# One large store of zeros written as two large and fifteen small stores, ahead of the last group's dv store

## The chip, the cores and the metric

The kernel runs on one core of a Trainium2 chip. The metric is the device time of one execution in microseconds; the median of the runs is compared. The core has five engines that work side by side: TensorE (PE in the profile) for matrix products, VectorE (DVE), ScalarE (ACT), GpSimd (POOL) and SyncE (SP), which here only issues transfers. Transfers between the main memory (HBM) and the on-chip memory (SBUF) are DMAs; sixteen DMA engines of the core carry them out.

## The reference

A decode step of one token for four sequences: layer norm, then in parallel an attention over a window of a key/value cache and a gated feed-forward network, both added to the input. The kernel computes the output and the gradients of all inputs for a given gradient of the output.

```python
def ref(x, k_cache, v_cache, wq, wo, w_gate, w_up, w_down):   # x: (4, 1, 512)
    xn = layernorm(x)
    W = 1024                                   # of 4096 cached positions, the last ones
    q = heads(xn @ wq)                         # 32 query heads of 128, 8 key/value heads
    k, v = last(k_cache, W), last(v_cache, W)  # (4, 8, 1024, 128), each shared by 4 heads
    o = softmax(q @ k.T * 128**-0.5) @ v
    a = o @ wo
    b = (gelu(xn @ w_gate) * (xn @ w_up)) @ w_down
    return x + a + b
out, vjp = jax.vjp(ref, ...)
return (out, *vjp(grad_out))
```

The gradients of the caches, dk and dv, have the caches' full shape (4, 8, 4096, 128) in bf16, 33.6 MB each. Outside the window of the last 1,024 positions they are zero, so three quarters of each, 3,072 positions per sequence and head, are zeros that still have to be written: 50.3 MB of the 81.0 MB that the kernel writes.

## The kernel before

The feed-forward part comes first: its weights are loaded, transposed by TensorE, and its weight gradients computed and stored from tiles named osb_d and osb_g. Then the attention runs in a loop over four groups t of two key/value heads each (NT = 4, GP = 2). For a group, `kv_steps` transposes the keys (later the values) and forms the scores, `softmax` and `softmax_d` work out the softmax and its gradient in pieces, `odq` computes the outputs and the query gradients, and `fin` adds to the sums for the output and for dx. The key and value gradients of a group are made by `dvdk` (tiles stg_dv, stg_dk), those of the two attention weights by `dw` (tiles osb_o, osb_q). These last two are cut into pieces: a product, a copy out of PSUM (line 97 on ScalarE, line 98 on VectorE) and, with the last piece of a tile, a store. The pieces wait in a queue `bg`; `tick(n)`, called between the steps of the main path, runs n of them. What is left over after the last group is run by `tick(len(bg))`, line 754 before the change.

The order of the instructions on every engine is the order of the program text; nothing is moved by a scheduler. All large stores are issued by SyncE through `store` (lines 100 to 107). A store of dv or dk waits until its tile is filled, and while it waits, SyncE issues nothing that comes after it. The tile pool `stage` holds three stg tiles of 8 KB in each partition; each tile is 1 MB. A fourth tile takes the place of the first, and so its filling waits until the first one's store has landed. Per group four such tiles are made: two of dv, two of dk.

The zeros come from one SBUF tile, ztile, 128 partitions of 12 KB. `zero(n)` takes n entries off `zlist` and writes for each a region of one sequence and two heads: 128 rows of 12 KB, 1,536 KB. There are 32 such regions. They are spread over the program as filling for the DMA engines: three at the start, single ones after other stores (each dv and dk store is followed by one, line 490), four in a row in the last group (lines 733 and 734), and what remains at the end (line 755).

Semaphores are set by the framework. For hardware DMAs it uses eight completion counters in turn, for SyncE's and ScalarE's DMAs together in the order of the program. A DMA that takes a counter for the next time first waits until the DMA that had it before, the eighth before it, has landed. In the compiled program every store on SyncE from the ninth DMA on has such a wait. The two small results, out_b (line 769) and dx_b (line 787), are stored by ScalarE.

Around the change SyncE's order is: the two osb_q stores of group 2, the four zero stores, the first dv store of group 3, a zero store, the second dv store, a zero store, the first dk store, a zero store, osb_o, the second dk store, a zero store, osb_o, two osb_q, and two zero stores that end the program.

Of the kernel before, what the change touches and what calls it, by code (L numbers as in the profile page):

```python
# [14 lines left out]
P = 128  # L15
# [3 lines left out]
def kernel(  # L19
# [28 lines left out]
    nc = tc.nc  # L48

    B, Sq, D = A_x.shape  # L50
    _, G, Sk, Dh = A_k_cache.shape
# [4 lines left out]
    K0 = Sk - W  # L56
# [43 lines left out]
    def store(eng, out, in_, kind):  # L100

        eng.nop()
        d = eng.dma_start(out=out, in_=in_)
        for k in ("rest", "zeros") if kind == "rest" else ("rest",):
            tc.declare_no_dep(d.ins, group=k, reason="stores write disjoint parts of the outputs")
        tc.add_to_no_dep_group(kind, d.ins)
        return d
# [12 lines left out]
    def load_w(t, eng=nc.gpsimd):  # L120
        pool = w_pool[t % 2]
        wo_t[t] = pool.tile([P, HG, D], BF16, name="wo_sb", tag="wo")
        eng.dma_start(out=wo_t[t][:], in_=wo_v[t])
        wq_t[t] = pool.tile([P, ND, CW], BF16, name="wq_sb", tag="wq")
        eng.dma_start(out=wq_t[t][:], in_=wq_v[t])

    def load_kv(t, k):
        if t >= NT:
            return
        d_, src, nm = ((k_t, A_k_cache, "kb"), (v_t, A_v_cache, "vb"))[k]  # L130
        for g in range(GP):
            tl = kv_pool[t % 2].tile([P, JB, Dh], BF16, name=nm, tag=nm)
            nc.sync.dma_start(out=tl[:].rearrange("p j d -> p (j d)"),
                              in_=src[:, t * GP + g, K0:Sk, :].rearrange("b (m j) d -> m b (j d)", j=JB))
            d_[(t, g)] = tl
# [20 lines left out]
    ZR = 2  # L156
    ZW = K0 * Dh * ZR // P
    ztile = const.tile([P, ZW], BF16, name="ztile")
    zlist = deque((og, b, g) for b in range(B) for g in range(0, G, ZR) for og in (out_2, out_3))

    def zero(n=1):
        for _ in range(min(n, len(zlist))):
            og, b, g = zlist.popleft()
            store(nc.sync, og[b, g:g + ZR, 0:K0, :].rearrange("g (m j) d -> m g (j d)", m=P // ZR), ztile[:], "zeros")


    nc.gpsimd.memset(ztile[:], 0.0)
    zero(3)
    ident_f = const.tile([P, P], FP32, name="ident_f")
    nc.vector.tensor_copy(out=ident_f[:], in_=ident[:])  # L170
# [91 lines left out]
    def tick(n):  # L262
        for _ in range(min(n, len(bg))):
            bg.popleft()()
# [3 lines left out]
    def link(n=1):  # L268
        for _ in range(min(n, len(chain))):
            chain.popleft()()  # L270
# [64 lines left out]
    def kv_steps(t, k, links):  # L335

        zt = (qm_all, dom_all)[k][t % 2]
        blks = (k_t, v_t)[k]
        ps = ps_a.tile([P, WQ], FP32, name="S_ps", tag=("S", "dP")[k])
        st[t][("S", "dP")[k]] = ps[:]  # L340

        def mm(g, q, T_sb):
            c0 = SL - 1 - (g * NQ + q)
            for b in range(B):
                nc.tensor.matmul(ps[b * RB:(b + 1) * RB, :], lhsT=zt[:, b * GP + g, c0:c0 + RB],  # L345
                                 rhs=T_sb[:].rearrange("p (x b) -> p b x", b=B)[:, b, :], start=(g == 0 and q == 0),
                                 stop=(g == GP - 1 and q == NQ - 1), tile_position=(0, b * RB))

        last = None
        for g in range(GP):  # L350
            for q in range(NQ):
                T_ps = transposes([blks[(t, g)][:, q * JQ + j, :] for j in range(JQ)], "T")
                T_sb = tsb.tile([P, JQ * P], BF16, name="T_sb", tag="T")
                evac(T_sb[:], T_ps[:].rearrange("p j x -> p (j x)"), 1024, half=True)
                tick(1)
                link(links)
                if last:
                    mm(*last)
                last = (g, q, T_sb)
                tick(1)  # L360
                link(links)
        mm(*last)
# [104 lines left out]
    def odT(t, k):  # L467
        rows = st[t][("o", "dq")[k]]
        T_ps = transposes([rows[:, g, :] for g in range(GP)], "odT")
        rT = attw.tile([P, GP, B, rep], BF16, name="od_T", tag=f"od_T{k}")  # L470
        for g in range(GP):
            nc.vector.tensor_copy(out=rT[:, g].rearrange("p b r -> p (b r)"), in_=T_ps[:, g, g * 32:g * 32 + B * rep])
        st[t][("oT", "dqT")[k]] = rT
# [206 lines left out]
    for f4 in range(NF4):  # L680
        held = {}
        n = min(4, NF - 4 * f4)
# [34 lines left out]
    with tc.tile_pool(name="kv_b", bufs=GP, reuse_waits="tile") as kv_b, \  # L717
            tc.tile_pool(name="w_b", bufs=1, reuse_waits="tile") as w_b, \
            tc.tile_pool(name="stage", bufs=3, reuse_waits="tile") as stage:
        kv_pool[1], w_pool[1] = kv_b, w_b  # L720
        zero()
        pre(0)
        load_w(1)
        load_kv(1, 0)
        for t in range(NT):
            kv_steps(t, 0, 0)
            if t == 0:
                zero()
                load_kv(1, 1)
                zero()  # L730
            softmax(t)
            kv_steps(t, 1, 1)
            if t == NT - 1:
                zero(4)
            link(len(chain))
            softmax_d(t)
            link()
            odq(t, 0)
            load_kv(t + 2, 1)
            if t + 1 < NT:  # L740
                pre(t + 1)
            link(len(chain))
            odT(t, 0)
            odq(t, 1)
            load_kv(t + 2, 0)
            tick(2)
            odT(t, 1)
            fin(t)
            if t + 2 < NT:
                load_w(t + 2)  # L750
            (k0, k1), (o0, o1, q0, q1) = dvdk(t, 1), dw(t)
            for p in (k0, o0, k1, o1, q0, q1):
                bg.extend(p)
        tick(len(bg))
        zero(len(zlist))

        fin_ps = []
        for o in range(2):
            f_ps = ps_w.tile([B, ND, P], FP32, name="f_ps", tag="w")
            for c in range(ND):  # L760
                nc.tensor.transpose(f_ps[:, c, :], acc[:, o, c, :], ident_f[:])
            fin_ps.append(f_ps)
        acc_o = fin_ps[0][:].rearrange("b c p -> b (c p)")
        acc_d = attw.tile([B, P, ND], FP32, name="acc_d", tag="P_s")
        nc.vector.tensor_copy(out=acc_d[:].rearrange("b p c -> b c p"), in_=fin_ps[1][:])
        acc_d = acc_d[:].rearrange("b p c -> b (p c)")
        out_b = attw.tile([B, D], BF16, name="out_b", tag="pT")
        nc.vector.tensor_tensor(out=out_b[:], in0=acc_o, in1=x4[:], op=ALU.add)
        nc.scalar.dma_start(out=out_0.rearrange("b s d -> (b s) d"), in_=out_b[:])

        s1 = attw.tile([B, 1], FP32, name="s1", tag="m")
        nc.vector.reduce_sum(out=s1[:], in_=acc_d, axis=AX.X)
        pr = attw.tile([B, D], FP32, name="pr", tag="dS_s")
        s2 = attw.tile([B, 1], FP32, name="s2", tag="es")
        nc.vector.tensor_tensor_reduce(out=pr[:], in0=acc_d, in1=xn_f[:], scale=1.0, scalar=0.0,
                                       op0=ALU.mult, op1=ALU.add, accum_out=s2[:])
        nm1 = attw.tile([B, 1], FP32, name="nm1", tag="rr")
        nc.vector.tensor_scalar(out=nm1[:], in0=s1[:], scalar1=-1.0 / D, scalar2=None, op0=ALU.mult)
        nm2 = attw.tile([B, 1], FP32, name="nm2", tag="gs")
        nc.vector.tensor_scalar(out=nm2[:], in0=s2[:], scalar1=-1.0 / D, scalar2=None, op0=ALU.mult)  # L780
        nc.vector.scalar_tensor_tensor(out=pr[:], in0=xn_f[:], scalar=nm2[:, 0:1], in1=acc_d,
                                       op0=ALU.mult, op1=ALU.add)
        nc.vector.tensor_scalar(out=pr[:], in0=pr[:], scalar1=nm1[:, 0:1], scalar2=rstd[:, 0:1],
                                op0=ALU.add, op1=ALU.mult)
        dx_b = attw.tile([B, D], BF16, name="dx_b", tag="E_f")
        nc.vector.tensor_tensor(out=dx_b[:], in0=pr[:], in1=dy4[:], op=ALU.add)
        nc.scalar.dma_start(out=out_1.rearrange("b s d -> (b s) d"), in_=dx_b[:])
# [30 lines left out]
```

## Time and profile before

| | us |
|---|---|
| median of 2 runs | 283.31 (283.26 to 283.36) |
| the profiled execution, its own time | 283.0 |
| its span, first to last instruction | 281.0 |
| TensorE busy | 203.1 (72%) |
| VectorE busy | 164.1 (58%) |
| ScalarE busy | 117.8 (42%) |
| bytes moved by the DMA engines | 112.12 MB, 399 GB/s over the span |
| HBM read and written | 30.68 MB and 81.01 MB |

All times in the profile count from the first instruction of the profiled execution. The page cuts the span in 40 slices of 7.03 us and gives the busy share of each engine in tenths; its row DMA is the mean over the sixteen DMA engines. "SPq" marks what SyncE's sequencer does, such as issuing a DMA. A DMA is issued at one time and lands later: when all sixteen DMA engines have reported. "Packets" are the single pieces that one DMA engine moves, one row of a tile as a rule. The chain of waits follows the work that ended last back from the end, step by step, to what released it.

### The profile page before, as it was taken

Reading aid. Unit: us, or ns where it says so; the run is one execution under the profiler, and the core shown is the slowest. Engines: PE = TensorE matmul, PEld = TensorE weight load, DVE = VectorE, ACT = ScalarE, POOL = GpSimd, SP = SyncE. Lnnn points to the kernel's source line nnn. Section 1 sums busy time; section 2 is a strip of 40 time slices with the busy share of each in tenths; the row PEclk is TensorE's granted clock in tenths of the full one; section 3 lists DMA queues with packets and bytes.
Section 4 is the critical chain, followed back from the end, with each engine's and each line's share of the span. In section 5 each row is a group of like instructions: output and inputs, shape, how many; then the busy total and the mean of one; then the engine's idle time right before and its main releaser. Section 6 shows DMA issues by size and latency. Waiting matters only on the chain.

```text
span 281.0 us, 6867 instructions
## 1 busy us (share of the span) xinstructions
PE 203.1 (72%) x2972; PEld 138.8 (49%) x2972; DVE 164.1 (58%) x313; ACT 117.8 (42%) x219; POOL 40.1 (14%) x40
## 2 busy tenths in 40 slices
PE   0276699959789889998999299898999599390000
PEld 0265476735456665566775156677556484140000
DVE  7946646645776655577666067767677728386000
ACT  2030386635035418764448056443866038370000
POOL 8600000007002150002250000223000400000000
PEclk9999589986999999999999969999999979977555
DMA  7999999999999999999999999999999999999990
GB/s 264 393 375 431 431 426 417 425 419 424 369 395 424 422 420 420 426 415 422 419 417 411 412 424 423 431 383 398 385 368 415 387 432 410 425 429 422 398 422 30
DMA packets 19565, 112.12 MB, mean 399 GB/s; under 512 B 1664, under 2 KB 4496, under 8 KB 11088
## 3 DMA queue, kind: packets, MB, share of 16 engines
q1 hardware_dynamic: 17744, 103.56, 89.6%
q0 software_dynamic: 1632, 6.29, 5.6%
q10 hardware_dynamic: 160, 1.84, 1.9%
q8 instruction: 23, 0.38, 0.5%
q14 instruction: 6, 0.05, 0.0%
HBM read 30.68 MB, written 81.01 MB: 397 GB/s over the span
## 4 chain that ended last, share of the span: by engine, by line
PE 47%; DMA 22%; DVE 16%; ACT 4%; issue 2%; SPq 0%; DVEq 0%; ACTq 0%
DMA out_dram<-stg_dv 13%; PE T_ps L279 8%; PE kv_ps L484 7%; DMA wd_sb<-in_B_w_down_dram 6%; PE S_ps L345 5%; PE od_ps L450 5%; DMA out_dram<-osb_g 4%; DVE T_sb L98 3%; DVE dS_s L367 2%; PE wdT_ps L279 2%; PE dwq_ps L520 2%; PE acc_ps L256 2%; PE dwd_ps L660 2%; DVE P_s L367 2%; PE wgT_ps L279 2%
## 5 line engine op out<-in xcount | busy, mean ns | idle before, releaser
L98 DVE COPY T_sb<-T_ps 128x1024 bf16<-128x1024 bf16 x64 | 44.1, 688 | 26.7 <-PE T_ps L279 26.5
L97 ACT CAST stg_dk<-kv_ps 128x512 bf16<-128x512 f32 x52 | 29.2, 588 | 31.2 <-PE kv_ps L484 12.4
L97 ACT CAST stg_dv<-kv_ps 128x512 bf16<-128x512 f32 x51 | 28.1, 588 | 24.9 <-PE kv_ps L484 24.3
L484 PE MATMUL kv_ps<-qmr,dS_s 128*128 128x512 bf16 x64 | 23.9, 414 | 11.3 <-ACT stg_dk L97 10.6
L463 POOL TENSOR_TENSOR o_s<-od_r,msk_r 128x512 bf16<-128x512 bf16 x8 | 9.1, 1157 | 110.2 <-DVE od_r L455 80.9
L484 PE MATMUL kv_ps<-domr,P_s 128*128 128x512 bf16 x64 | 21.3, 382 | 0.0
L279 PE MATMUL T_ps<-ident,vb 128*128 128x128 bf16 x256 | 20.3, 225 | 0.4 <-DVE T_sb L98 0.4
L279 PE MATMUL T_ps<-ident,kb 128*128 128x128 bf16 x256 | 20.4, 225 | 0.0
L279 PEld LDWEIGHTS <-kb 128*128 128x128 bf16 x256 | 17.5, 101 | 4.5 <-issue 1.3
L279 PEld LDWEIGHTS <-vb 128*128 128x128 bf16 x256 | 17.2, 101 | 5.0 <-issue 3.2
L97 ACT CAST osb_q<-dwq_ps 128x512 bf16<-128x512 f32 x25 | 14.6, 587 | 8.3 <-PE dwq_ps L520 7.4
L329 POOL TENSOR_TENSOR domr<-r,msk 128x1024 bf16<-128x1024 bf16 x4 | 7.6, 1892 | 71.2 <-DVE r L326 65.1
L97 ACT CAST osb_g<-dwg_ps 128x512 bf16<-128x512 f32 (+1 forms) x25 | 12.3, 544 | 12.3 <-PE dwg_ps L673 6.3
L97 ACT CAST osb_o<-dwo_ps 128x512 bf16<-128x512 f32 x24 | 13.9, 586 | 4.5 <-PE dwo_ps L505 2.9
L98 DVE CAST stg_dk<-kv_ps 128x512 bf16<-128x512 f32 x12 | 8.0, 688 | 12.0 <-DMA out_dram<-stg_dv 11.2
L98 DVE COPY wgT<-wgT_ps 128x1024 bf16<-128x1024 bf16 x14 | 9.6, 686 | 6.8 <-PE wgT_ps L279 6.8
L345 PE MATMUL S_ps<-T_sb,qm 128*32 128x256 bf16 x128 | 12.7, 387 | 0.6 <-DVE T_sb L98 0.5
L345 PE MATMUL S_ps<-T_sb,dom 128*32 128x256 bf16 x128 | 12.7, 388 | 0.1
L505 PE MATMUL dwo_ps<-dyr,o_s 128*128 128x512 bf16 x32 | 12.4, 413 | 0.3 <-ACT stg_dk L97 0.2
L98 DVE COPY woT<-woT_ps 128x1024 bf16<-128x1024 bf16 x16 | 11.0, 686 | 2.7 <-PE woT_ps L279 2.3
L484 PEld LDWEIGHTS <-dS_s 128*128 128x128 bf16 x64 | 6.2, 101 | 12.2 <-issue 11.1
L520 PE MATMUL dwq_ps<-od_r,xnm 128*128 128x256 bf16 x64 | 11.6, 274 | 0.3 <-ACT osb_q L97 0.2
(188 smaller groups left out, 385.0 us busy)
## 6 DMA issues: line engine op xcount, KB each, us to landing
out_dram<-ztile SPq DMA_DIRECT2D x32, 1536.0 KB, 18.1
kb<-in_A_k_cache_dram SPq DMA_DIRECT2D x8, 1024.0 KB, 17.4
vb<-in_A_v_cache_dram SPq DMA_DIRECT2D x8, 1024.0 KB, 20.7
out_dram<-stg_dv SPq DMA_DIRECT2D x8, 1024.0 KB, 13.0
out_dram<-stg_dk SPq DMA_DIRECT2D x8, 1024.0 KB, 20.8
out_dram<-osb_o SPq DMA_DIRECT2D x8, 512.0 KB, 17.4
out_dram<-osb_q SPq DMA_DIRECT2D x8, 512.0 KB, 13.8
out_dram<-osb_g SPq DMA_DIRECT2D x8, 448.0 KB, 14.3
```

The source lines that it names most:

```text
L97: return nc.scalar.copy(out=out, in_=in_)
L98: return nc.vector.tensor_copy(out=out, in_=in_)
L256: nc.tensor.matmul(ps[:, c, :], lhsT=lf(c), rhs=rhs, start=(k == 0), stop=(k == len(terms) - 1))
L279: nc.tensor.transpose(ps[:, i, :], a, ident[:])
L329: nc.gpsimd.tensor_tensor(out=mr[:].rearrange("p g q d -> p (g q) d"), in0=r4[:, k, :].unsqueeze(1).broadcast_to([P, SL, Dh]), in1=msk[:]. ...
L345: nc.tensor.matmul(ps[b * RB:(b + 1) * RB, :], lhsT=zt[:, b * GP + g, c0:c0 + RB], rhs=T_sb[:].rearrange("p (x b) -> p b x", b=B)[:, b, :] ...
L367: nc.vector.scalar_tensor_tensor(out=out[:], in0=src[:].unsqueeze(2).broadcast_to([P, WQ, B]), scalar=rr[:, 0:1], in1=mskb[:].unsqueeze(1) ...
L450: nc.tensor.matmul(od_ps[g * 32:g * 32 + B * rep, k, g, :], lhsT=cols[:, jj, g * NQ + q, :], rhs=blks[(t, g)][:, j, :], start=(j == 0), st ...
L463: nc.gpsimd.tensor_tensor(out=o_s[:, g], in0=rows[:, g].unsqueeze(1).broadcast_to([P, rep, Dh]), in1=msk_r[:].unsqueeze(2).broadcast_to([P ...
L484: nc.tensor.matmul(mps[:].rearrange("p q d -> p (q d)"), lhsT=src[:, j * P:(j + 1) * P], rhs=mr[:, g].rearrange("p q d -> p (q d)"), start ...
L505: nc.tensor.matmul(mps[:], lhsT=o_s[:, g].rearrange("p r d -> p (r d)")[:, i:rep * Dh:rep], rhs=dyr[:], start=True, stop=True)
L520: nc.tensor.matmul(mps[:, i].rearrange("p g d -> p (g d)"), lhsT=xnm[:, i2 * 2 + i, c * P:(c + 1) * P], rhs=dq_r[:].rearrange("p g d -> p ...
```

## The change

One of the four zero regions ahead of the first dv store of the last group, the fourth, is written in other pieces. The region has two heads of 768 KB. The first head is written as 64 rows of 12 KB. The second head's positions from 480 on are written as 96 rows of 6.75 KB (648 KB), and its first 480 positions, 120 KB, by 15 stores of 15, 14, ... 1 rows of 1 KB each. All take their zeros from the same tile, all are issued by SyncE in this order, and the same bytes are written as before. Everything else in the program stays as it is.

```diff
+    def zero_steps():
+
+        og, b, g = zlist.popleft()
+        store(nc.sync, og[b, g, 0:K0, :].rearrange("(m j) d -> m (j d)", m=P // ZR), ztile[0:P // ZR], "zeros")
+        store(nc.sync, og[b, g + 1, 480:K0, :].rearrange("(m j) d -> m (j d)", m=96), ztile[0:96, 0:27 * Dh], "zeros")
+        r = 0
+        for n in range(15, 0, -1):
+            store(nc.sync, og[b, g + 1, r * 4:(r + n) * 4, :].rearrange("(m j) d -> m (j d)", m=n), ztile[0:n, 0:4 * Dh],
+                  "zeros")
+            r += n
...
             if t == NT - 1:
-                zero(4)
+                zero(3)
+                zero_steps()
             link(len(chain))
```

## The prediction

> **What bounds the kernel now.** I began with the slices of the span, which show whether an engine or the transfers fill it (40 slices of 7.03 us; each digit is a busy share in tenths).
>
> ```profile
> PE   0276699959789889998999299898999599390000
> DMA  7999999999999999999999999999999999999990
> GB/s 264 393 375 431 431 426 417 425 419 424 369 395 424 422 420 420 426 415 422 419 417 411 412 424 423 431 383 398 385 368 415 387 432 410 425 429 422 398 422 30
> ```
>
> TensorE has finished by slice 36, yet the DMA row stays at 9 to slice 38, at 400 to 430 GB/s. The transfers set the end; time in which they stand still is lost. Next come the last stretches, from the table of stretches (PE, PEld, DVE, ACT, POOL busy, clock, DMA share, GB/s):
>
> ```profile
> 268.00:275.00 7.00, 0.00 (x0) 0.00 (x0) 0.00 (x0) 0.00 (x0) 0.00 (x0) 0.50 0.89 377
> 275.00:281.00 6.00, 0.00 (x0) 0.00 (x0) 0.00 (x0) 0.00 (x0) 0.00 (x0) 0.50 0.04 18
> ```
>
> In the last one no compute engine works and the DMA share is 0.04, about one of 16 engines. The packet records say why: fifteen DMA engines end at 274.4 to 275.5, one at 279.57, in an unbroken row of 12 KB packets. That lag is 4.2 to 4.6 us in every large store from 233 us on; it is old backlog, not a slower pace. So the path that sets the end is the last DMA engine's queue, and the question is what the change does to that queue. Then SyncE's timeline (start, duration), since every large store is issued there:
>
> ```profile
> 219.31 0.38 SPq L103 DMA_DIRECT2D out_dram<-osb_q  x1
> 219.74 4.40 SPq L103 DMA_DIRECT2D out_dram<-ztile  x4
> 233.63 0.54 SPq L103 DMA_DIRECT2D out_dram<-stg_dv  x1
> 234.21 1.39 SPq L103 DMA_DIRECT2D out_dram<-ztile  x1
> ...
> 242.94 0.54 SPq L103 DMA_DIRECT2D out_dram<-ztile  x1
> ```
>
> The x4 are the four zero stores that the change touches. After them SyncE waits for data, and the first dv store goes at 233.63. Behind it other zero stores queue up, one of them held until 242.94. What held that one is a completion counter: in the compiled program SyncE's DMAs use eight counters in turn, so a store on SyncE waits for the store eight places before it (the two small outputs of ScalarE take turns too). The store at 242.94 shares its counter with the fourth zero store, whose sixteenth completion is recorded at 242.92: issued at 222.77, 20.1 us to landing. Last, the chain of waits around dv:
>
> ```profile
> 233.63 11.70 DMA out_dram<-stg_dv
> 245.32 0.02 issue
> ...
> 245.42 0.59 ACT stg_dk L97
> ```
>
> The first dv store lands at 245.32 on the last engine; the second dk piece needs its stage buffer, so the compute chain hangs on it as well.
>
> [...] The trace shows SyncE idle from 224.1 to 233.6 while the queues drain. [...] Here the 4-row load of x, on empty queues, was issued at 0.81 and complete by 2.24, so 1.4. [...] 201.19 to a first packet at 202.39 and 209.76 to 210.97, both 1.20.
>
> **The change part by part.** Bytes are unchanged: 768 + 648 + 120 = 1,536 KB. One store becomes 17, so 16 issues are added on SyncE, all ahead of dv. No compute instruction changes. Because 16 is two rounds of eight, later stores keep their counters; what changes is which store each waits for. Call the two large parts A (64 rows) and B (96 rows), and the small ones s15 to s1 by rows. Eight places back: s15 waits for osb_o, s14 and s13 for the two osb_q, s12, s11, s10 for the other three zero stores, s9 for A, s8 for B, s7 for s15, and so on to s1 for s9. The dv store now waits for s8.
>
> Hence seven small stores (84 KB) are all that can be queued behind B. s8 can't be issued until B has landed on all 16 engines, and dv is the ninth issue after that. Behind the waiting SyncE stand dv, its zero store and all later stores.
>
> - *B lands.* Before, the last of the four lands at 242.92. In each engine 96 KB become 48 + 40.5 KB, four packets of 460 ns and six of about 0.26 us (pro rata from 309 ns for 8 KB), 3.4 instead of 3.7 us. B lands at about 242.7 on the last engine (238.4 on the others).
> - *Eight small issues, s8 to s1.* The nearest rows are the 4-row DMAs: 389 and 266 ns on SyncE (x, dy), 529 and 264 on ScalarE (out_b, dx_b), and 0.04 us between issues. From below 8 x 0.30 = 2.4 us, from above 8 x 0.57 = 4.6. The second of each pair is the cheap one, so a row of them should be near the floor; I take 0.35 each, 2.8 us. A gain is excluded: these issues can't start earlier. With 0.1 us of waking, dv is issued at 245.6. Do the completions bind? [...] s1 likewise finds s9 landed, whose 1 KB packets (46 ns each) follow B.
> - *Restart.* First packet 1.2 us later: 246.8.
> - *Against before.* There the last engine started dv as soon as it had the fourth zero store's data behind it, 242.55 (completion is 0.36 later, as at the end: last packet 279.57, landed 279.94). So the last engine's queue slips by 246.8 - 242.55 = 4.2 us. The other fifteen stand still for about 8.5 us, but 4.3 of that is slack they had.
> - *The first seven small stores* (s15 to s9) cost nothing: they are issued while A and B drain. Without that cover they would cost 7 x 0.35 = 2.5 us.
> - *Compute chain.* dv lands 8 packets of 309 ns and 0.36 after 246.8, at 249.6, 4.3 later than before; so the second dk, osb_o, osb_q and dx_b all come 4.3 later. What is next late? The last two zero stores wait for dx_b's counter: 263.25 before, 267.5 then. The engines would run dry only when osb_q is written, 272.3 + 4.2 = 276.5. Nine microseconds are left, so no second stop.
> - *After the restart.* Both dv stores and the first dk store, each with a zero store behind it, are ready by then; a pair takes about 1.1 us to issue and 6.3 to move (2.6 MB at 418 GB/s), so the queues stay full.
>
> Sum: the remaining 15.7 MB take 37.0 us (242.55 to 279.57 before, unbroken), now from 246.8: 283.8, landed 284.1, and the closing 1.1 us: span 285.2 against 281.0. The profiled execution took 283.0, so 287.2; it lies 0.3 below the median of 283.31 (which moves by 0.1 us), so on the median 287.5. I put 287.4, 1.4% more.
>
> **Rivals.**
>
> 1. *Dear small issues.* If a store of 1 to 8 rows costs what out_b's did (0.53 + 0.04), or completions bind one after the other, eight take 4.6 us and the slip is 6.0: 289.3. For it: two of the four known issues are over 0.38. Against: dy and dx_b at 0.265 include the same work.
> 2. *A second stop* in the tail, because out_b and dx_b come later and osb_q and the last zero stores wait for their counters: 1 to 2 us more, 289 to 290. Against: the nine microseconds above. It speaks for it that fifteen engines, once 4.3 us ahead, now lie level with the last one, which takes nothing from that margin.
> 3. *Not slower: the backlog is gone in time.* If B lands so early that s8 to s1 are issued before dv's data is ready, the new waits are all covered and nothing slips: 283.3. It decides at 233.63 - 2.8 = 230.8 for B's landing. The trace has 242.9, twelve microseconds too late; only if four zero stores were written 12 us faster, or if the counters didn't hold as the store at 242.94 shows. The change failing to do what it says amounts to this too.
>
> **How the numbers follow.** Forecast 0.80, rival 1 0.12, rival 2 0.04, rival 3 0.04. The forecast's own span is a slip of 3.5 (0.28 per issue) to 5 us, 286.8 to 288.3. To hold 8 in 10 with the unknown issue price in it, I go to 286.3 below (a restart quicker than 1.2 us) and 289.3 above. Two per cent, about what a measurement of this kernel can tell from no change, is 288.98; I count rivals 1 and 2 as above it: faster 0.01, same 0.83, slower 0.16.
>
> **What would show it.** In the profile after: the DMA row drops in slices 34 and 35 (239 to 246 us), one engine alone from 238.4 to 242.7 and then none; SyncE has s8 to s1 in one row right after B's landing, dv at about 245.6, and waits of L103 for a zero store grow by some 10 us; the wait of stg_dk's evacuation for the dv store grows from 4.6 to about 9; at the end all 16 engines finish together, without the 4.4 us tail on one. If small issues take 0.5 us or more, the step "eight small issues" is wrong; if dv is issued near 233.6, the counters are; if the DMA row drops again after 250, the tail is.

## The result, and the profile after

The changed kernel takes 291.62 us in the median (291.37 to 291.87) against 283.31 before. The ratio is 1.0293, with a 95% interval of 1.0249 to 1.0338: 8.3 us slower, where 4.1 were forecast and 6.0 were the upper end. The profiled execution took 291.87 with a span of 289.9 us, 8.9 more than before.

The slices of the changed kernel (one slice is 7.25 us here) show the standstill that was forecast, but longer and with a slow stretch ahead of it:

```profile
PE   0275799959788889898996599889995992080000
...
DMA  7999999999999999999999999999999991499997
GB/s 268 388 380 429 435 415 428 420 420 398 376 422 408 412 420 420 424 423 426 409 408 419 422 432 419 393 411 378 400 398 386 428 235 43 203 418 417 413 407 320
```

In the slice of 235 GB/s the DMA row still reads 9. The DMA engines are busy there, and yet move little more than half of what they moved before. The table of stretches parts the two things; its columns are start and end, length, busy time of PE, PEld, DVE, ACT, POOL, clock, DMA share, GB/s. First the changed kernel:

```profile
226.00:233.00 7.00, 6.84 (x121) 5.32 (x117) 3.18 (x8) 3.98 (x8) 0.00 (x0) 0.92 1.05 418
233.00:240.00 7.00, 6.48 (x53) 2.81 (x52) 6.14 (x11) 5.71 (x12) 0.00 (x0) 1.00 0.87 199
240.00:247.00 7.00, 0.87 (x4) 0.19 (x3) 0.29 (x1) 0.40 (x1) 0.00 (x0) 0.80 0.10 31
247.00:250.00 3.00, 0.00 (x0) 0.00 (x0) 0.00 (x0) 0.00 (x0) 0.00 (x0) 0.50 0.05 12
250.00:257.00 7.00, 2.60 (x7) 0.92 (x7) 2.89 (x5) 2.25 (x4) 0.00 (x0) 0.50 0.95 393
```

The same stretches of the kernel before:

```profile
233.00:240.00 7.00, 6.48 (x56) 2.86 (x54) 5.92 (x10) 5.88 (x12) 0.00 (x0) 1.00 1.02 422
240.00:247.00 7.00, 2.25 (x8) 0.77 (x7) 2.25 (x4) 1.74 (x4) 0.00 (x0) 0.90 0.99 416
```

From 233 to 240 us the share is 0.87 and the rate 199 GB/s: slow transfers. From 240 to 247 the share is 0.10, between one and two of the 16 engines, and from 247 to 250 it is 0.05, less than one: the standstill. SyncE's timeline and the chain of waits of the changed kernel say what held dv:

```profile
219.61 29.60 SPq L103 DMA_DIRECT2D out_dram<-ztile  x20
249.32 0.55 SPq L103 DMA_DIRECT2D out_dram<-stg_dv  x1
249.91 0.60 SPq L103 DMA_DIRECT2D out_dram<-ztile  x1
```

```profile
223.96 22.69 DMA out_dram<-ztile
246.66 0.02 issue
246.67 0.28 SPq L103
246.95 0.04 issue
246.99 0.30 SPq L103
...
248.96 0.25 SPq L103
...
249.32 4.35 DMA out_dram<-stg_dv
253.67 0.02 issue
...
253.77 0.59 ACT stg_dk L97
```

The 96-row store was issued at 223.96 and landed at 246.66. Eight small issues follow at once, each 0.25 to 0.30 us with 0.04 between, and dv goes out at 249.32. The chain has the form that the prediction gave it, but its first link ends 4.0 us later than forecast (242.7).

### The profile page after: what moved, and what is told of

It reads as the page before. It is cut to its first block, busy times and chain, and to the rows that moved or that the text cites. A ratio compares the mean times of both kernels' runs of the same rounds, so it can differ in the third digit from the quotient of the medians.

```text
span 289.9 us, 6873 instructions
## 1 busy us (share of the span) xinstructions
PE 202.5 (70%) x2962; PEld 138.7 (48%) x2972; DVE 164.1 (57%) x313; ACT 117.9 (41%) x219; POOL 40.1 (14%) x40
## 3 DMA queue, kind: packets, MB, share of 16 engines
q10 hardware_dynamic: 160, 1.84, 1.8%
## 4 chain that ended last, share of the span: by engine, by line
PE 41%; DMA 27%; DVE 15%; ACT 3%; SPq 3%; issue 2%; DVEq 0%; ACTq 0%
DMA out_dram<-stg_dv 10%; PE T_ps L290 8%; DMA out_dram<-ztile 8%; PE kv_ps L495 6%; DMA wd_sb<-in_B_w_down_dram 5%; PE S_ps L356 5%; DMA out_dram<-osb_g 4%; PE od_ps L461 3%; DVE T_sb L98 3%; SPq L103 2%; PE dwq_ps L531 2%; PE wgT_ps L290 2%; PE dwd_ps L671 2%; DVE P_s L378 2%; PE dwo_ps L516 2%
## 5 line engine op out<-in xcount | busy, mean ns | idle before, releaser
L495 PE MATMUL kv_ps<-qmr,dS_s 128*128 128x512 bf16 x62 | 22.9, 404 | 19.8 <-ACT stg_dk L97 19.2
L495 PE MATMUL kv_ps<-domr,P_s 128*128 128x512 bf16 x58 | 19.9, 387 | 0.1
```

The costliest lines, as they stand in the source:

```text
L495: nc.tensor.matmul(mps[:].rearrange("p q d -> p (q d)"), lhsT=src[:, j * P:(j + 1) * P], rhs=mr[:, g].rearrange("p q d -> p (q d)"), start ...
```

## The experiments

At first two things were open: whether the slow stretch came from the SBUF partitions that the 64-row store reads (0 to 63), from its destination and row shape, or from the small stores; and whether the drained counters cost what was forecast. In the ratios each kernel is compared with the kernel before on the same chip.

P is the theory that the source partitions made the slow stretch: the 64-row store is slow because it reads partitions 0 to 63, and what else is under way beside it is slowed too. P1 and P2 are two narrower forms of it: by P1 the loss comes from the engine that lags, slowed while it still reads an ordinary zero store, by P2 from the half rate of the 64-row store itself. H is the rival that the stretch came from elsewhere. The profile names neither the partition nor the engine of a packet, so the runs test these only by what they lead to; why the partitions should matter was not shown.

**Other partitions for the 64-row store.**

```diff
-        store(nc.sync, og[b, g, 0:K0, :].rearrange(...), ztile[0:P // ZR], "zeros")
+        store(nc.sync, og[b, g, 0:K0, :].rearrange(...), ztile[32:32 + P // ZR], "zeros")
```

> The changed kernel with one edit: the 64-row store reads its zeros from partitions 32 to 95 instead of 0 to 63. Theory P[...]: its packets take 0.46 us again instead of 0.95, the 96-row store lands near 243 instead of 246.7, dv is issued near 246 and the time falls to 287 to 288.8. Rival H (the slow stretch comes from the destination, one head of 64 rows, or from the many small stores): no change, 291.6.

Measured: 288.14 us, ratio 1.0179 (1.0156 to 1.0202). Nothing but the source partitions of one store differs from the changed kernel, and 3.5 us are gone (3.2 by the ratios). In the packet records from 232.5 to 242.5 us, 1 of 101 packets of 12 KB takes over 0.7 us, against 55 of 81 in the changed kernel: 24 of those take 0.9 to 1.0, and 22 more, up to 2.1. The destination is cleared. SyncE's timeline of this kernel:

```profile
220.19 25.81 SPq L103 DMA_DIRECT2D out_dram<-ztile  x20
246.10 0.58 SPq L103 DMA_DIRECT2D out_dram<-stg_dv  x1
```

The 96-row store landed at 243.44 and dv was issued at 246.10 (forecast for the change: 242.7 and 245.6). So with the partitions put right, the steps of the prediction hold, and 288.14 lies in its range.

**The small stores in one.** In place of the fifteen:

```diff
-        r = 0
-        for n in range(15, 0, -1):
-            store(... ztile[0:n, 0:4 * Dh], "zeros")
-            r += n
+        store(nc.sync, og[b, g + 1, 0:480, :].rearrange("(m j) d -> m (j d)", m=96), ztile[0:96, 0:5 * Dh], "zeros")
```

> The changed kernel with the 15 small stores written as one store of 96 rows of 1.25 KB; the 64-row store still reads partitions 0 to 63. Theory P: dv is issued near 233.6 again, no standstill, but the slow stretch from about 232 us stays, with 0.95 us packets of the 64-row store; 285.5 to 287.3. Rival H in its second form (small stores make the stretch slow): no slow stretch, 283.3. If the drained counters were the whole loss: 283.3 as well.

Measured: 288.96 us, ratio 1.0216 (1.0186 to 1.0246). dv is issued early again and nothing stands still, yet the slow stretch is there:

```profile
232.71 0.55 SPq L103 DMA_DIRECT2D out_dram<-stg_dv  x1
...
233.00:240.00 7.00, 6.33 (x49) 2.64 (x48) 5.95 (x11) 5.63 (x11) 0.00 (x0) 1.00 0.97 229
240.00:247.00 7.00, 0.56 (x2) 0.16 (x2) 0.00 (x0) 0.00 (x0) 0.00 (x0) 0.74 1.01 373
```

(The first line is of SyncE's timeline, the others of the table of stretches.) So the small stores don't make it. But the loss, 5.9 us, is above the upper end of 287.3 that I had worked out from a half rate for this store: half rate alone was too small a sum.

**Both edits.**

> Both edits together: partitions 32 to 95 for the 64-row store and one store in place of the 15 small ones. Theory P with the counters: nothing is left of either loss, 283.2 to 284. Rival H in its first form (the destination in 64 rows is slow): still 285 or more.

Measured: 284.97 us, ratio 1.0072 (1.0046 to 1.0098). Most of both losses is gone, but not all: 1.95 us stayed, more than expected. With the changed kernel and the two runs before, the two losses stand in a square: the partitions of the 64-row store cost 4.0 us without the small stores (288.96 to 284.97) and 3.5 with them (291.62 to 288.14); the small stores cost 3.2 us with good partitions and 2.7 with bad ones. The changed kernel was timed beside other runs of the kernel before; by the ratios the two figures that use it are 3.2 and 2.2.

**Seven small stores behind the 96-row store.** Good partitions, and the 36 rows of the stores of 8 to 1 rows put into one store ahead of the 64-row store:

```diff
+        store(nc.sync, og[b, g + 1, 336:480, :].rearrange("(m j) d -> m (j d)", m=36), ztile[0:36, 0:4 * Dh], "zeros")
...
-        for n in range(15, 0, -1):
+        for n in range(15, 8, -1):
```

> As the first run (partitions 32 to 95), but only the stores of 15 to 9 rows stand behind the 96-row store; the 36 rows of the other eight are one store ahead of the 64-row store. Theory of the counters: dv waits for the 96-row store itself and is issued right when it lands, near 243; the queues then stand still for 1.3 us alone, and the time is 2.7 us (eight issues of 0.34) below the first run, 284.7 to 286. If the seven stores ahead of the drain cost something too, or the small stores are slow in transfer: 287 or more.

Measured: 286.07 us, ratio 1.0103 (1.0082 to 1.0124), 2.1 below the first run where 2.7 were expected, and so just above the expected 286; in the profiled executions the spans differ by 2.9 us (286.7 to 283.8) and the issue of dv by 2.8.

```profile
219.93 21.97 SPq L103 DMA_DIRECT2D out_dram<-ztile  x13
243.28 0.56 SPq L103 DMA_DIRECT2D out_dram<-stg_dv  x1
```

The 96-row store landed at 243.21, and dv went at 243.28. So eight issues behind the drain, the wait until the 96-row store has landed, are what the last eight small stores cost. The issues of the seven ahead of it are covered. But seven are enough to make dv wait for the 96-row store, so the queues still run empty and dv's first packet comes 1.2 us after its issue, at 244.49: this kernel is still 3.05 us slower than the one before.

**Partitions 64 to 127.** From the run with merged small stores I drew a narrower theory, P1. Of the sixteen DMA engines one lags by some 4 us: the third zero store of the kernel before landed on it at 239.16, on the others by 235.06. When the others start on the 64-row store, this one still reads rows of the zero store before it. If the others, reading partitions 0 to 63, slow that, it is this engine, which sets the end, that loses as a bystander. That 64 rows from partitions 64 to 127 would leave it alone, although that store would be just as slow itself, was an assumption of mine, which this run tests:

```diff
-        store(nc.sync, og[b, g, 0:K0, :].rearrange(...), ztile[0:P // ZR], "zeros")
+        store(nc.sync, og[b, g, 0:K0, :].rearrange(...), ztile[64:64 + P // ZR], "zeros")
```

> The changed kernel with the 64-row store reading partitions 64 to 127. [...] Theory P1[...]: packets of the 64-row store still take 0.95 us, but the lagging engine is left alone, the 96-row store lands near 243.5, and the time is that of partitions 32 to 95, 287.5 to 288.8. Theory P2 (the store's own half rate is what costs): 291.6, as with partitions 0 to 63.

Measured: 288.14 us, ratio 1.0165 (1.014 to 1.0191), the same as with partitions 32 to 95. The transfers, however, are slow again: the engines are busy for 0.87 of the stretch, as in the changed kernel, and move 244 GB/s, where the run with partitions 32 to 95 (second line) moved as much in 0.71.

```profile
233.00:240.00 7.00, 6.48 (x59) 2.96 (x57) 5.98 (x11) 5.88 (x12) 0.00 (x0) 1.00 0.87 244
...
233.00:240.00 7.00, 6.48 (x60) 3.04 (x59) 5.98 (x11) 5.88 (x12) 0.00 (x0) 1.00 0.71 246
```

From 232.5 to 242.5 us, 47 of 101 packets of 12 KB take over 0.7 us. But the zero store ahead of it lands on the last engine at 240.16, not at 242.97, and the 96-row store at 243.66, not at 246.66. The last engine's own packets can be followed back, each beginning within 0.03 us of the end of the one before. The last four of that zero store take 0.47 to 0.48 us each here; in the changed kernel they took 1.78, 1.35, 0.80 and 0.88. So the bystander is there in the trace. The slow store cost nothing here against the run with partitions 32 to 95 (288.14 us both), where it slowed only engines that have slack.

**The rest of 1.95 us.** Both edits, and the two 96-row stores read partitions 32 to 127 instead of 0 to 95:

```diff
-        store(nc.sync, og[b, g + 1, 480:K0, :].rearrange(...), ztile[0:96, 0:27 * Dh], "zeros")
-        store(nc.sync, og[b, g + 1, 0:480, :].rearrange(...), ztile[0:96, 0:5 * Dh], "zeros")
+        store(nc.sync, og[b, g + 1, 480:K0, :].rearrange(...), ztile[32:128, 0:27 * Dh], "zeros")
+        store(nc.sync, og[b, g + 1, 0:480, :].rearrange(...), ztile[32:128, 0:5 * Dh], "zeros")
```

> As the kernel with both edits (partitions 32 to 95, one store of 96 rows in place of the small ones), which took 1.95 us more than the kernel before, with the two 96-row stores reading partitions 32 to 127 instead of 0 to 95. P1 says that the rest came from these two[...], the lagging engine is spared, 283.0 to 283.8. If the rest had another source (more stores, 6.75 KB rows): 285 again.

Measured: 283.58 us, ratio 1.0001 (0.9989 to 1.0013). The rest is gone, so it too hung on the source partitions: the same region in three stores can be free. How it arose is another matter. With both edits the large 96-row store took the lagging engine 3.02 us (landings at 241.31 and 244.33), here 1.78 (240.97 and 242.75), and in both runs the other engines had by then gone on to dv and the zero store behind it. The lagging engine was thus slowed in its own reading of the 96-row store, and not as a bystander of it. Why partitions 0 to 95 slow it and 32 to 127 do not is not shown.

**Source partitions alone, twice.** The region as two stores of 64 rows, without small stores, from partitions 0 to 63 and then from 32 to 95:

```diff
-        store(... ztile[0:P // ZR], "zeros")          # and the 96-row and fifteen small stores
+        for h in range(ZR):
+            store(nc.sync, og[b, g + h, 0:K0, :].rearrange("(m j) d -> m (j d)", m=P // ZR), ztile[0:64], "zeros")
```

> The zero region as two stores of 64 rows of 12 KB, one for each head, both reading partitions 0 to 63; no small stores. P1: [...] 286.6 to 290.2, more than one such store cost (4.0). P2, half rate alone: 1,536 KB in 7.3 instead of 3.7 us, 286.7. [...]

> The same two stores of 64 rows, both reading partitions 32 to 95[...], 282.8 to 283.5. A loss here would be that of splitting the region or of its rows in HBM.

Measured: 287.66 us, ratio 1.0143 (1.0115 to 1.0171), and 283.06 us, ratio 0.9992 (0.998 to 1.0004). The same bytes in the same rows to the same places; the source partitions alone make 4.6 us. The stretch of the first and then of the second:

```profile
233.00:240.00 7.00, 6.48 (x53) 2.81 (x52) 6.14 (x11) 5.70 (x12) 0.00 (x0) 1.00 1.01 213
```

```profile
233.00:240.00 7.00, 6.48 (x57) 2.91 (x55) 5.98 (x11) 5.88 (x12) 0.00 (x0) 1.00 1.02 421
```

The first run's time doesn't tell the bystander from half rate (286.7 were expected by half rate and 286.6 to 290.2 for the bystander, the latter an estimate of mine whose working no run shows); the run with partitions 64 to 127 does. Its trace shows the lagging engine slow in its own share of the two stores, too: they took it 3.45 and 3.93 us (landings at 240.83, 244.28 and 248.21), in the second run 1.91 and 1.85 (238.97, 240.88 and 242.73). No kernel here beats the one before by more than its interval.

## Why the prediction was wrong

- *What bounds the kernel*: right. The last DMA engine's queue sets the end; whatever delays it moves the end. Its lag was read a little too narrowly: it is 4.0 us in the first dv store (241.35 to 245.32), not 4.2 to 4.6 throughout. No sum hangs on that.
- *The counters*: right. The store of 8 rows went out when the 96-row store had landed, and dv eight issues after that; the store of 8 rows, whose counter dv takes over, had landed at 248.16, 1.5 us after its issue at 246.67 and before dv's turn.
- *B lands at 242.7*: **wrong, the step that failed.** The sum starts from the last engine coming to the 64-row store when it came to the fourth zero store before, with the third landed on it at 239.16: what the new store does to a transfer that is still in flight was put at nothing, without a reason. The third zero store landed on it at 242.97. It took the last engine 7.07 us (from the landing of the second), against 3.82 before and 3.83 with partitions 64 to 127; another 0.5 us of delay stood there already when the first zero store landed (231.91; 231.42 before, 232.14 with partitions 32 to 95), ahead of the slow stretch, and is not explained. Then 64 and 96 rows took it 1.87 and 1.82 us, where 1.84 and 1.56 were in my working. So the 460 ns that I gave the packets of the 64-row store were right on this engine, which was alone by then, and wrong on the others, where 0.95 was common. The term was +4.0 us. I had asked only on how many engines a store of 64 rows runs, and there it is like one of 128: 16 completions are recorded for each of the two. What I left out is which partitions it reads: two stores of 64 rows moved 213 GB/s from partitions 0 to 63 and 421 from 32 to 95 (233 to 240 us). That such a store also slows another one beside it, the third zero store shows.
- *How large the bystander's loss is*: the third zero store took the last engine 3.2 us longer than with partitions 64 to 127 (7.07 against 3.83). This is measured; through what one engine slows another is not shown.
- *Eight small issues at 0.35*: right, 2.65 us in all (246.67 to 249.32) for 2.9 expected. Rival 1, dear issues, has fallen; its 289.3 is nearer to the measured time, but for a wrong reason.
- *Restart 1.2 us*: right, dv is issued at 249.32 and its first packet is at 250.52. The figure came from the two dk stores of group 2 in the trace of before: issued at 201.19 and 209.76, first packets at 202.39 and 210.97.
- *The remaining 15.7 MB in 37.0 us*: 0.9 short. From 250.52 to the last packet at 288.46 it is 37.9 without a break; the first dv store already takes 0.3 of that (3.15 us from its first packet to its landing, 2.8 in the working). The longer tail belongs to the standstill: it takes 37.9 to 38.0 us in all four kernels whose queues ran empty, while in the six others the last engine needs 37.0 to 37.1 from the landing of the region's last store to the end. After a standstill all 16 engines run level, where before the last one ran its final 4.4 us alone. I didn't test whether that is the cause.
- *Rival 2, a second stop*: fell; the stretches from 250 to 285 us hold 393 to 424 GB/s. *Rival 3, not slower*: fell with the landing at 246.66.

The sum closes for the profiled execution: 4.2 forecast, +4.0 for the landing, -0.2 for the issues, +0.9 for the tail, 8.9 us of span. The rest of what the prediction priced, it had nearly right: with good partitions the change costs 5.1 us, of which about 0.9 is the longer tail.

## What to carry to other kernels

Before a store of fewer than 128 rows is called free, look at which partitions it reads: 64 rows from partitions 32 to 95, twice, cost nothing here (283.06 us, ratio 0.9992), while 64 rows from partitions 0 to 63 cost 3.2 to 4.0 us more than the same rows from 32 to 95. Where DMA engines are not level, price a transfer by what it does to the one that lags, in its own share and in what that engine is still reading: the slow store from partitions 64 to 127 left it alone and took no longer than one from 32 to 95 (288.14 us both). And before a long wait, don't leave a row of tiny transfers in the counters' window: here it emptied the queues (12 GB/s from 247 to 250 us), and each of the last eight cost its issue time of 0.3 us.

## What the runs showed of the hardware that I had not expected

- Packets of 12 KB take 0.46 us in the stores of 128 rows (the median of 4,096 in the kernel before). While the 64-row store from partition 0 ran, 24 of 81 took 0.9 to 1.0 us, and 22 took longer, up to 2.1.
- A slow store is slow for others too: an ordinary 128-row zero store in flight on the lagging engine took 7.07 us there instead of 3.82.
- While the lagging engine was behind by 4.4 us at the end of the kernel before, the standstill made all engines level; in the changed kernel the sixteen completions of the last store lie within 0.3 us (288.49 to 288.81).
- A store of 1 to 8 rows of 1 KB is issued in 0.25 to 0.30 us and, on empty queues, complete 1.1 to 1.4 us after its issue (248.96 to 250.06 for the 1-row one, 246.99 to 248.35 for the 7-row one); the 8-row one, queued on the lagging engine too, took 1.5. On the lagging engine, the small stores queued there completed 0.19 us apart.
